# Spread reads on SyncE's queue, product sums dealt out over wave slots, attention of two batches at fixed waves

## The chip, the cores and the metric

The kernel runs on one core of one Trainium2 chip. The metric is the device time of a whole execution in microseconds: 318.45 us before the change, the median of 3 runs (317.96 to 318.91). The core has a matrix engine (TensorE, PE in the profile, with its weight loads as PEld), VectorE (DVE), ScalarE (ACT), GpSimd (POOL) and SyncE (SP), which here only issues transfers. Matrix products are written to PSUM, all other tiles lie in SBUF.

## The reference

Two blocks run one after the other. The first is an attention whose weights are products of two small projections. The second is a gated feed-forward layer.

```python
# attention: q, k, v are (4, 4, 1088, 32); S1, S2 are (8, 32)
a = np.einsum('rd,bhsd->bhsr', S1, x)            # phi(x), for x = q and x = k
b = np.einsum('rd,bhsd->bhsr', S2, x)
phi = np.einsum('bhsi,bhsj->bhsij', a, b).reshape(*x.shape[:-1], 64)
kv  = np.einsum('bhsf,bhsd->bhfd', k_p, v)
num = np.einsum('bhsf,bhfd->bhsd', q_p, kv)
den = np.einsum('bhsf,bhf->bhs', q_p, k_p.sum(axis=2))[..., None] + 1e-06
attn = num / den
# feed-forward: x is (4352, 128); w_gate, w_val are (128, 1536); w_out is (1536, 128)
x = attn.transpose(0, 2, 1, 3).reshape(4352, 128)
out = (1 / (1 + np.exp(-(x @ w_gate))) * (x @ w_val)) @ w_out
```

## The kernel before

**Feed-forward part.** The 4352 tokens are cut into chunks of 512 (numbers 0 to 7) and one of 256 (number 8). The 1536 hidden columns are cut into 12 blocks of 128. One *wave* (`w1`, matmuls at L457) multiplies a chunk by the gate and value weights of one block; ScalarE takes the sigmoid of the gate half (L465), and VectorE multiplies it with the value half (`glu`, L487, tile g). Waves write to a PSUM tile with two buffers. A chunk has 12 waves (chunk 8 has 6, of two blocks each), and waves are counted through all chunks: `moe["n"]`.

Chunks 1 to 7 form the product with w_out by a scheme of seven half-size products in place of eight (as Strassen and Winograd do it), over pairs of blocks. For each pair of waves GpSimd forms sums of the two g (`token_sums`, L328 to L335, tile tsum), and sums of the weights stand ready in ws. PE then runs four products into one accumulator in PSUM (`w2_a`, tag acc0) and three into another (`w2_b`, tag acc1), all at L339. There is one buffer for each tag. `w2_a` of a pair is put three, and `w2_b` four wave slots after that of the pair's second wave. After the last pair of a chunk, the results are combined: ScalarE copies the upper halves of each accumulator to SBUF (L401, L428), VectorE adds (L402 and L405 from acc0; L429 to L432 from acc1 and from tiles in SBUF), turns the result (L436, tile o_sb), and SyncE stores it (`store`, L353).

Chunks 0 and 8 use the plain product instead (`w2`, L370), into acc0 as their numbers are even.

**The order of work** is written out by hand. The order in the program is the order on each of the four compute engines. `slot(group, waves)` first emits a piece of attention work, and then, for each of so many waves: the `glu` of the wave before, the products that are due, and the matmuls of the next wave:

```python
        for _ in range(waves):
            ...
            glu()
            while todo and todo[0][0] <= moe["n"]:
                todo.pop(0)[1]()
            if more:
                w1()
```

The sums of a chunk's end are emitted inside the last `w2_a` and the last `w2_b`, behind the products.

**Attention part.** Batch 0 is done ahead of the waves. For batches 1 to 3 the pieces are, in order: `turn_k`, `turn_q` (transposes on VectorE, L536, L547), `begin` (projections kps and cqps on PE, then `spread`), `outer` twice (L646), `sum_z` twice (L822), `kv_all` (kvz on PE), `qmult` twice (L766, needs the tiles qp and bq), `weights_z` (L897 to L904), `ndt`, and `parts` (den_j, nps and the division, which writes the tokens xT that later waves read). Before, a loop over the batches puts one wave (batch 1) or two waves (batches 2 and 3) between the pieces.

`spread(b, ns, cq, put, get)` writes the projected queries cq to a DRAM tile dq (queue `put`) and reads them back in other layouts: six reads into qp and bq (queue `get`, L738) and eight into the small tiles a8 and b8 (queue `put`, L759). For batches 1 to 3 `put` is SyncE and `get` is GpSimd.

Of the kernel before, what the change touches and what calls it, by code (L numbers as in the profile page):

```python
# [12 lines left out]
ALU = mybir.AluOpType  # L13
# [7 lines left out]
def kernel(  # L21
# [282 lines left out]

    xT = const.tile([P, NTOK], F32, tag="xT")

    moe = {"sum": -1, "ci": 0, "w": 0, "n": 0, "ready": 0, "acc": None, "gate": None, "todo": []}

    def fast(ci):
        return 0 < ci < len(tok_chk) - 1 and tok_chk[ci][1] == TCH  # L310
# [77 lines left out]
    def w2_a(ci, i, g, t):  # L388
        if i == 0:
            moe["sum"] = ci  # L390
            fst["a"] = pso.tile([P, TCH], F32, tag="acc0", name="prod")
        lo, hi = fst["a"][:64], fst["a"][64:]
        w, first, last = w_sb[:, 2], i == 0, i == NJ // 2 - 1
        product(lo[:, :HALF], w[:, 2 * i, :64], g[:, 0, :HALF], first, last)
        product(hi[:, :HALF], w[:, 2 * i + 1, :64], g[:, 1, :HALF], first, last)
        product(lo[:, HALF:], ws[:, 3, i], g[:, 1, HALF:], False, last)
        product(hi[:, HALF:], ws[:, 1, i], t[:, 2], False, last)
        if last:
            e = fst["e"] = raw.tile([P, 2, 2, HALF], F32, tag="w_in", name="other")[:64]
            r = fst["r"] = raw.tile([P, 5, HALF], F32, tag="w_in", name="res")[:64]  # L400
            nc.scalar.copy(out=e[:, 0], in_=hi.rearrange("p (u x) -> p u x", u=2))  # L401
            nc.vector.tensor_tensor(  # L402
                out=ends(r, 1, 3), in0=twice(lo[:, :HALF]), in1=e[:, 0], op=ALU.add
            )
            nc.vector.tensor_tensor(out=r[:, 2], in0=lo[:, HALF:], in1=r[:, 4], op=ALU.add)  # L405

    def twice(x):
        return bass.AP(tensor=x.tensor, offset=x.offset, ap=[list(x.ap[0]), [0, 2], [1, HALF]])

    def ends(r, u, step):  # L410
        x = r[:, u]
        return bass.AP(
            tensor=x.tensor, offset=x.offset, ap=[list(x.ap[0]), [step * HALF, 2], [1, HALF]]
        )

    def w2_b(ci, i, g, t):
        if i == 0:
            fst["b"] = pso.tile([P, TCH], F32, tag="acc1", name="prod")
        lo, hi = fst["b"][:64], fst["b"][64:]
        w, first, last = w_sb[:, 2], i == 0, i == NJ // 2 - 1  # L420
        p5 = (lo[:, :HALF], ws[:, 0, i], t[:, 0], first, last)
        p4 = (hi[:, :HALF], w[:, 2 * i + 1, 64:], t[:, 3], first, last)
        p7 = ((hi if i % 2 else lo)[:, HALF:], ws[:, 2, i], t[:, 1], False, i >= NJ // 2 - 2)
        for p in (p4, p5, p7) if i % 2 else (p5, p4, p7):
            product(*p)
        if last:
            e, r = fst["e"], fst["r"]
            nc.scalar.copy(out=e[:, 1], in_=hi.rearrange("p (u x) -> p u x", u=2))  # L428
            nc.vector.tensor_tensor(out=r[:, 0], in0=lo[:, HALF:], in1=e[:, 1, 1], op=ALU.add)  # L429
            nc.vector.tensor_tensor(out=r[:, 4], in0=r[:, 4], in1=r[:, 0], op=ALU.add)  # L430
            nc.vector.tensor_tensor(out=r[:, 3], in0=r[:, 4], in1=e[:, 1, 0], op=ALU.subtract)
            nc.vector.tensor_tensor(  # L432
                out=ends(r, 2, 2), in0=twice(lo[:, :HALF]), in1=ends(r, 2, 2), op=ALU.add
            )
            o_sb = sbA.tile([P, 2, TCH // 32, 32], F32, tag="o_sb", name="o_sb")
            nc.vector.transpose(  # L436
                out=o_sb[:64].rearrange("p d t x -> p (d t x)"),
                in_=r[:, 1:].rearrange("p u x -> p (u x)"),
            )
            store(ci, lambda g4: o_sb[32 * (g4 % 2) : 32 * (g4 % 2) + 32, g4 // 2])  # L440

    def w1():

        ci = moe["ci"]
        t0, tw = tok_chk[ci]
        jn = TCH // tw
        j0 = moe["w"] * jn
        wv = psm.tile([P, 2, TCH], F32, tag="wave", name="wave")

        tp = tw // 2 if ci == 0 and j0 == 0 else tw  # L450
        turn = (moe["w"] // 2) % 2
        for o in range(0, tw, tp):
            for which in range(2):
                for jj in range(jn):
                    for c in (0,) if ci == 0 else (1 - turn, turn):
                        d = slice(0, P) if ci == 0 else slice(64 * c, 64 * c + 64)
                        nc.tensor.matmul(  # L457
                            out=wv[d, which, jj * tw + o : jj * tw + o + tp],
                            lhsT=w_sb[:, which, j0 + jj, d],
                            rhs=xT[:, t0 + o : t0 + o + tp],  # L460
                            start=True,
                            stop=True,
                        )
        sg = sbG.tile([P, TCH], F32, tag="sg", name="sg")
        nc.scalar.activation(out=sg, in_=wv[:, 0], func=ACTF.Sigmoid)  # L465
        if ci == 0:
            if j0 == 1:
                narrow_01(2, 3)
            if 0 < j0 < NJ - 2:
                narrow_w(j0 + 1, 3)  # L470
            narrow_w(j0 + 2, 1)
            narrow_w(j0 + 2, 2)
            if j0 < 3:
                narrow_w(j0 + 3, 0)
            if j0 > 1:
                narrow_w(j0 + 4, 0)
            if j0 == NJ - 3:
                weight_sums(0, NJ // 4)
        if ci == 1 and j0 == 1:
            weight_sums(NJ // 4, NJ // 2)  # L480
        if moe["w"] % 2 == 0:
            moe["g"] = sbG.tile([P, 2, TCH], F32, tag="g", name="g")
        pair, odd, n = moe["g"], moe["w"] % 2, moe["n"]

        def glu():
            g = pair[:, odd]
            nc.vector.tensor_tensor(out=g, in0=wv[:, 1], in1=sg, op=MUL)  # L487
            todo = moe["todo"]
            if not fast(ci):
                lag = 3 if ci else 2  # L490
                part = (ci, j0, jn, g.rearrange("p (j t) -> p j t", j=jn))
                todo.append((n + lag, lambda: w2(*part)))
            elif odd:
                part = (ci, j0 // 2, pair, token_sums(pair))
                todo.append((n + 3, lambda: w2_a(*part)))
                todo.append((n + 4, lambda: w2_b(*part)))

        moe["gate"] = glu
        moe["w"] += 1
        moe["n"] += 1  # L500
        if j0 + jn == NJ:
            moe["ci"] += 1
            moe["w"] = 0

    def glu():
        if moe["gate"] is not None:
            moe["gate"]()
            moe["gate"] = None

    def slot(group, waves):  # L510

        if group is not None:
            group()
        todo = moe["todo"]
        for _ in range(waves):
            more = moe["ci"] < len(tok_chk)
            if more and sum(tok_chk[moe["ci"]]) > moe["ready"]:
                break
            glu()
            while todo and todo[0][0] <= moe["n"]:  # L520
                todo.pop(0)[1]()
            if more:
                w1()
            elif not todo:
                break
            else:
                todo.pop(0)[1]()
# [236 lines left out]
    def qmult(b, n):  # L764
        q0 = half(QP[b], n)
        nc.vector.tensor_tensor(out=q0, in0=q0, in1=half(BQ[b], n), op=MUL)  # L766
# [368 lines left out]
    def begin(b):  # L1135
        glu()
        kps(b)
        cq[b] = qcomp(b, (0, 1), (psm, "wave"))
        spread(b, (0, 1), cq[b], nc.sync, nc.gpsimd)

    def q01():
        spread(0, (1,), qcomp(0, (1,), (ps2, "two")), nc.scalar, nc.sync)
# [24 lines left out]
    def kv_all(b):  # L1167
        kv(b, ZS[b])
        kvd(b)
# [8 lines left out]
    slot(lambda: part01(lambda: narrow_w(NJ - 1, 3)), 1)  # L1178
    slot(last01, 1)
    v_t[1] = load_v(1)  # L1180
    for b in range(1, B):
        more = b + 1 < B
        wn = 1 if b == 1 else 2
        turn_k(b)
        if b > 1:
            turn_q(b, 0)
        slot(None, wn)
        if b == 1:
            turn_q(b, 0)
        turn_q(b, 1)  # L1190
        slot(lambda: begin(b), 1)
        for pi in range(2):
            outer(b, pi)
            slot(None, wn)
        for step in range(2):
            sum_z(b, step)
            slot(None, wn)
            if b == 1 and step == 0:
                masks()
        slot(lambda: kv_all(b), wn)  # L1200
        if more:
            v_t[b + 1] = load_v(b + 1)
        qmult(b, 0)
        weights_z(b)
        slot(lambda: ndt(b), 1)
        qmult(b, 1)
        load_kq(b + 1)
        if b == 1:
            slot(None, 1)
        slot(lambda: parts(b), wn + 5)  # L1210
    slot(None, 10**3)


# [28 lines left out]
```

## Time and profile before

| what | value |
|---|---|
| time, median of 3 runs | 318.45 us |
| profiled execution: span, mean granted PE clock | 318.3 us, 0.972 |
| waves L457 on PE | 820 records, 215.8 us busy |
| products L339 on PE | 588 records, 153.7 us busy (68.8 + 33.9 + 26.0 + 25.0) |
| g, L487 on VectorE | 102 of 684 ns, 69.7 us busy |
| token sums L328, L334, L335 on GpSimd | 42 each of 1377, 753 and 815 ns |
| chain that ended last | PE 64%, DVE 14%, POOL 10%, issue 6%, DMA 2%, ACT 2% |
| reads qp<-dq and bq<-dq on GpSimd's queue | 18, median 8.1 and 9.5 us from issue to landing |
| chunk sums on VectorE, mean of one | L402 681, L405 416, L429 411, L430 416, L431 416, L432 682, L436 1236 ns |

Busy time on PE overlaps with itself, as matmuls are pipelined. The clock is a share of full speed, as the throttle grants it. In the list of waits a row says which engine and line waited, for which engine and line, and gives the total in us, the number of times, and the longest. In the timeline a row gives the start in us, the duration, the engine, line and operation, the tiles (out<-in), the shapes, how many instructions were merged, and in brackets how long the engine was idle before it, and for whom.

### The profile page before, as it was taken

Reading aid. Unit: us, or ns where it says so; the run is one execution under the profiler, and the core shown is the slowest. Engines: PE = TensorE matmul, PEld = TensorE weight load, DVE = VectorE, ACT = ScalarE, POOL = GpSimd, SP = SyncE. Lnnn points to the kernel's source line nnn. Section 1 sums busy time; section 2 is a strip of 40 time slices with the busy share of each in tenths; the row PEclk is TensorE's granted clock in tenths of the full one; section 3 lists DMA queues with packets and bytes.
Section 4 is the critical chain, followed back from the end, with each engine's and each line's share of the span. In section 5 each row is a group of like instructions: output and inputs, shape, how many; then the busy total and the mean of one; then the engine's idle time right before and its main releaser. Section 6 shows DMA issues by size and latency. Waiting matters only on the chain.

```text
span 318.3 us, 5511 instructions
## 1 busy us (share of the span) xinstructions
PE 299.3 (94%) x2176; PEld 153.6 (48%) x2176; DVE 184.9 (58%) x310; ACT 88.8 (28%) x164; POOL 161.6 (51%) x196
## 2 busy tenths in 40 slices
PE   9899999499999889979999999899999999999995
PEld 3444432145454344533654455443555456545853
DVE  6997798817629546386255954795226422832361
ACT  2556523112124122230223312221223222322320
POOL 1456560954453694603546976434554655466300
PEclk9999999879999799995999999999999999999999
DMA  7994142963300394215000790002000200010021
GB/s 219 353 309 105 69 141 55 215 139 97 121 0 0 84 229 99 61 26 163 2 0 37 159 211 5 2 1 35 1 0 2 33 0 2 4 31 0 0 35 17
DMA packets 30553, 24.35 MB, mean 76 GB/s; under 512 B 20480, under 2 KB 25728, under 8 KB 30528
## 3 DMA queue, kind: packets, MB, share of 16 engines
q1 hardware_dynamic: 27024, 16.15, 19.1%
q0 software_dynamic: 2592, 7.08, 9.6%
q10 hardware_dynamic: 912, 0.77, 0.9%
q8 instruction: 17, 0.28, 0.4%
q14 instruction: 8, 0.07, 0.1%
HBM read 20.73 MB, written 3.26 MB: 75 GB/s over the span
## 4 chain that ended last, share of the span: by engine, by line
PE 64%; DVE 14%; POOL 10%; issue 6%; DMA 2%; ACT 2%; SPq 0%; POOLq 0%; ACTq 0%; DVEq 0%
PE wave L457 40%; PE prod L339 16%; POOL head L118 3%; POOL tsum L328 2%; PE moeout L370 2%; POOL ws L323 2%; DVE head L109 2%; DVE g L487 2%; PE nps L982 2%; DVE w_sb L127 1%; DVE o_sb L436 1%; POOL bq L738 1%; POOL tsum L334 1%; PE kvz L788 1%; DMA dq<-cq 1%
## 5 line engine op out<-in xcount | busy, mean ns | idle before, releaser
L457 PE MATMUL wave<-xT,w_sb 128*64 128x512 f32 (+3 forms) x820 | 215.8, 577 | 0.8 <-DVE g L487 0.8
L487 DVE TENSOR_TENSOR g<-wave,sg 128x512 f32<-128x512 f32 x102 | 69.7, 684 | 111.6 <-ACT sg L465 107.3
L457 PEld LDWEIGHTS wave<-xT,w_sb 128*64 128x64 f32 (+1 forms) x820 | 83.3, 143 | 71.0 <-issue 52.4
L465 ACT ACTIVATE sg<-wave 128x512 f32<-128x512 f32 x102 | 61.0, 598 | 196.4 <-PE wave L457 189.0
L328 POOL TENSOR_TENSOR tsum<-g 128x512 f32<-128x512 f32 x42 | 57.8, 1377 | 97.6 <-DVE g L487 97.6
L339 PE MATMUL prod<-tsum,ws 128*64 128x256 f32 x252 | 68.8, 391 | 6.6 <-POOL tsum L334 6.6
L339 PEld LDWEIGHTS prod<-tsum,ws 128*64 128x64 f32 x252 | 33.4, 140 | 21.6 <-issue 8.5
L335 POOL TENSOR_TENSOR tsum<-tsum,g 128x256 f32<-128x256 f32 x42 | 34.2, 815 | 3.3
L339 PE MATMUL prod<-g,w_sb 128*64 128x256 f32 x168 | 33.9, 382 | 0.1
L334 POOL TENSOR_TENSOR tsum<-tsum,g 128x256 f32<-128x256 f32 x42 | 31.6, 753 | 3.3
L339 PE MATMUL prod<-tsum,w_sb 128*64 128x256 f32 x84 | 26.0, 392 | 0.0
L339 PE MATMUL prod<-g,ws 128*64 128x256 f32 x84 | 25.0, 379 | 0.0
L339 PEld LDWEIGHTS prod<-g,w_sb 128*64 128x64 f32 x168 | 16.0, 137 | 18.1 <-issue 16.9
L118 POOL TENSOR_TENSOR head<-head,tail 128x384 int32<-128x384 int32 (+2 forms) x14 | 13.3, 953 | 18.0 <-DVE head L109 14.9
L370 PE MATMUL moeout<-g,w_sb 128*128 128x512 f32 (+1 forms) x48 | 18.9, 503 | 0.3 <-DVE w_sb L127 0.3
L339 PEld LDWEIGHTS prod<-tsum,w_sb 128*64 128x64 f32 x84 | 11.3, 139 | 7.8 <-issue 6.8
L339 PEld LDWEIGHTS prod<-g,ws 128*64 128x64 f32 x84 | 11.5, 137 | 3.3
L370 PEld LDWEIGHTS moeout<-g,w_sb 128*128 128x128 f32 x48 | 8.5, 189 | 8.3 <-issue 4.2
L646 DVE TENSOR_TENSOR kp<-kab 128x1152 f32<-128x1152 f32 (+2 forms) x10 | 11.3, 1144 | 0.0
L766 DVE TENSOR_TENSOR qp<-qp,bq 128x1152 f32<-128x1152 f32 (+1 forms) x7 | 9.1, 1296 | 0.0
L982 PE MATMUL nps<-qp,nd 64*32 64x256 f32 (+1 forms) x128 | 6.5, 465 | 2.6 <-DVE qp L766 2.3
L436 DVE STREAM_TRANSPOSE o_sb<-res 64x1024 f32<-64x1024 f32 x7 | 8.7, 1236 | 0.2
(114 smaller groups left out, 196.0 us busy)
## 6 DMA issues: line engine op xcount, KB each, us to landing
qp<-dq POOLq DMA_DIRECT2D x6, 576.0 KB, 8.1
bq<-dq POOLq DMA_DIRECT2D x12, 288.0 KB, 9.5
v<-in_v_dram SPq DMA_DIRECT2D x16, 144.0 KB, 3.9
kq<-in_k_dram SPq DMA_DIRECT2D x3, 544.0 KB, 4.1
kq<-in_q_dram SPq DMA_DIRECT2D x3, 544.0 KB, 5.0
w_in<-in_moe_w_out_dram SPq DMA_DIRECT2D x6, 256.0 KB, 7.1
w_in<-in_moe_w_gate_dram SPq DMA_DIRECT2D x5, 256.0 KB, 6.1
w_in<-in_moe_w_val_dram SPq DMA_DIRECT2D x5, 256.0 KB, 6.6
```

The lines of the kernel that those rows point to most:

```text
L118: nc.gpsimd.tensor_tensor(out=head, in0=head, in1=tail, op=ALU.add)
L328: nc.gpsimd.tensor_tensor(out=t[:, :2], in0=g.rearrange("p f (t x) -> p t f x", t=2)[:, 1], in1=g1, op=ALU.subtract,)
L334: nc.gpsimd.tensor_tensor(out=t[:, 2], in0=t[:, 1], in1=g1[:, 0], op=ALU.add)
L335: nc.gpsimd.tensor_tensor(out=t[:, 3], in0=t[:, 2], in1=g[:, 1, :HALF], op=ALU.subtract)
L339: nc.tensor.matmul(out=out, lhsT=lhsT, rhs=rhs, start=start, stop=stop, skip_group_check=True)
L370: nc.tensor.matmul(out=moe["acc"][:, :tw], lhsT=w_sb[:, 2, j, :], rhs=g[:, jj, :tw], start=(j == 0), stop=(j == NJ - 1),)
L436: nc.vector.transpose(out=o_sb[:64].rearrange("p d t x -> p (d t x)"), in_=r[:, 1:].rearrange("p u x -> p (u x)"),)
L457: nc.tensor.matmul(out=wv[d, which, jj * tw + o : jj * tw + o + tp], lhsT=w_sb[:, which, j0 + jj, d], rhs=xT[:, t0 + o : t0 + o + tp], sta ...
L465: nc.scalar.activation(out=sg, in_=wv[:, 0], func=ACTF.Sigmoid)
L487: nc.vector.tensor_tensor(out=g, in0=wv[:, 1], in1=sg, op=MUL)
L646: eng.tensor_tensor(out=KP[b][:, pi, j0:j1].rearrange("p j m (i l) -> p (j m) i l", i=R), in0=bass.AP(tensor=a0.tensor, offset=a0.offset, ...
L982: nc.tensor.matmul(out=t[32 * h : 32 * h + 32, c, :w], lhsT=ND[b][rows, 32 * h : 32 * h + 32], rhs=half(QP[b], n)[rows, 2 * (h % 2) + h // ...
```

## The change

It has three parts. The six reads of `spread` for batches 1 to 3 are issued by SyncE, so that GpSimd has no transfer to wait for or to issue. The sums at a chunk's end become a list of steps, `moe["late"]`, of which one is emitted in each wave slot, behind its `glu` and ahead of the products that are due; the aim is that VectorE has no long run of work in one slot. They are also regrouped: L431's subtraction comes first, the last two additions become one, and the transpose is done in two halves. Chunk 8's first product waits one slot longer. Third, the attention pieces of batches 2 and 3 are each put at a wave number (`plan`), apart from the ends of chunks; batch 1 keeps its order.

```diff
         if last:
...
-            nc.vector.tensor_tensor(
-                out=ends(r, 1, 3), in0=twice(lo[:, :HALF]), in1=e[:, 0], op=ALU.add
-            )
-            nc.vector.tensor_tensor(out=r[:, 2], in0=lo[:, HALF:], in1=r[:, 4], op=ALU.add)
+            def first_sums():
+                add(ends(r, 1, 3), twice(lo[:, :HALF]), e[:, 0])
+            def third():
+                add(r[:, 2], lo[:, HALF:], r[:, 4])
+            moe["late"] += [[first_sums], [third]]
...
-            nc.vector.tensor_tensor(out=r[:, 0], in0=lo[:, HALF:], in1=e[:, 1, 1], op=ALU.add)
-            nc.vector.tensor_tensor(out=r[:, 4], in0=r[:, 4], in1=r[:, 0], op=ALU.add)
-            nc.vector.tensor_tensor(out=r[:, 3], in0=r[:, 4], in1=e[:, 1, 0], op=ALU.subtract)
-            nc.vector.tensor_tensor(
-                out=ends(r, 2, 2), in0=twice(lo[:, :HALF]), in1=ends(r, 2, 2), op=ALU.add
-            )
...
+            def fourth():
+                add(r[:, 3], r[:, 4], e[:, 1, 0], op=ALU.subtract)
+            def fifth():
+                add(ends(r, 2, 2), twice(lo[:, :HALF]), ends(r, 2, 2))
+            def seventh():
+                add(r[:, 0], lo[:, HALF:], e[:, 1, 1])
+            def last_sums():
+                add(r[:, 3:5], r[:, 3:5], twice(r[:, 0]))
...
+            def turn_store():
+                turned(1)
+                store(ci, lambda g4: o_sb[32 * (g4 % 2) : 32 * (g4 % 2) + 32, g4 // 2])
+            moe["late"] += [[fourth, fifth, seventh], [last_sums], [lambda: turned(0)], [turn_store]]
...
-                lag = 3 if ci else 2
+                lag = 2 if ci == 0 else 3 if j0 else 4
...
             glu()
+            for step in moe["late"].pop(0) if moe["late"] else ():
+                step()
             while todo and todo[0][0] <= moe["n"]:
                 todo.pop(0)[1]()
...
-        spread(b, (0, 1), cq[b], nc.sync, nc.gpsimd)
+        spread(b, (0, 1), cq[b], nc.sync, nc.sync)
...
+    plan = {2: (27, 29, 30, 31, 32, 34, 36, 37, 38, 39, 42, 44)}
+    plan[3] = (48, 49, 51, 53, 56, 57, 58, 59, 60, 61, 63, 68)
+    for b in range(2, B):
+        at = iter(plan[b])
+        until(next(at))
         turn_k(b)
+        for n in range(2):
+            until(next(at))
+            turn_q(b, n)
+        until(next(at))
         slot(lambda: begin(b), 1)
...
```

More of the change, by code (lines that the diff above doesn't have):

```diff
@@ L305 @@
     xT = const.tile([P, NTOK], F32, tag="xT")
-    moe = {"sum": -1, "ci": 0, "w": 0, "n": 0, "ready": 0, "acc": None, "gate": None, "todo": []}
+    moe = {"sum": -1, "ci": 0, "w": 0, "n": 0, "ready": 0, "acc": None, "gate": None, "todo": [], "late": []}
     def fast(ci):
@@ L401, in w2_a, with add @@
             nc.scalar.copy(out=e[:, 0], in_=hi.rearrange("p (u x) -> p u x", u=2))
-            nc.vector.tensor_tensor(
-                out=ends(r, 1, 3), in0=twice(lo[:, :HALF]), in1=e[:, 0], op=ALU.add
-            )
-            nc.vector.tensor_tensor(out=r[:, 2], in0=lo[:, HALF:], in1=r[:, 4], op=ALU.add)
+            def first_sums():
[3 more added lines that the diff above has]
+            moe["late"] += [[first_sums], [third]]
+    def add(out, in0, in1, op=ALU.add):
+        nc.vector.tensor_tensor(out=out, in0=in0, in1=in1, op=op)
     def twice(x):
@@ L428, in w2_b, with turned @@
             nc.scalar.copy(out=e[:, 1], in_=hi.rearrange("p (u x) -> p u x", u=2))
-            nc.vector.tensor_tensor(out=r[:, 0], in0=lo[:, HALF:], in1=e[:, 1, 1], op=ALU.add)
-            nc.vector.tensor_tensor(out=r[:, 4], in0=r[:, 4], in1=r[:, 0], op=ALU.add)
-            nc.vector.tensor_tensor(out=r[:, 3], in0=r[:, 4], in1=e[:, 1, 0], op=ALU.subtract)
-            nc.vector.tensor_tensor(
-                out=ends(r, 2, 2), in0=twice(lo[:, :HALF]), in1=ends(r, 2, 2), op=ALU.add
-            )
-            o_sb = sbA.tile([P, 2, TCH // 32, 32], F32, tag="o_sb", name="o_sb")
[L436 to L440, printed above, removed]
+            o_sb = sbA.tile([P, 2, TCH // 32, 32], F32, tag="o_sb", name="o_sb")
+            def fourth():
[6 more added lines that the diff above has]
+                add(r[:, 3:5], r[:, 3:5], twice(r[:, 0]))
+            def turned(d):
+                nc.vector.transpose(
+                    out=o_sb[:64, d].rearrange("p t x -> p (t x)"),
+                    in_=r[:, 1 + 2 * d : 3 + 2 * d].rearrange("p u x -> p (u x)"),
+                )
+            def turn_store():
+                turned(1)
+                store(ci, lambda g4: o_sb[32 * (g4 % 2) : 32 * (g4 % 2) + 32, g4 // 2])
+            moe["late"] += [[fourth, fifth, seventh], [last_sums], [lambda: turned(0)], [turn_store]]
     def w1():
@@ L1180, with until @@
     v_t[1] = load_v(1)
-    for b in range(1, B):
-        more = b + 1 < B
-        wn = 1 if b == 1 else 2
-        turn_k(b)
[L1185 to L1190, printed above, removed]
+    turn_k(1)
+    slot(None, 1)
+    turn_q(1, 0)
+    turn_q(1, 1)
+    slot(lambda: begin(1), 1)
+    for pi in range(2):
+        outer(1, pi)
+        slot(None, 1)
+    for step in range(2):
+        sum_z(1, step)
+        slot(None, 1)
+        if step == 0:
+            masks()
+    slot(lambda: kv_all(1), 1)
+    v_t[2] = load_v(2)
+    qmult(1, 0)
+    weights_z(1)
+    slot(lambda: ndt(1), 1)
+    qmult(1, 1)
+    load_kq(2)
+    slot(None, 1)
+    slot(lambda: parts(1), 1)
+    def until(n):
+        slot(None, n - moe["n"])
+    plan = {2: (27, 29, 30, 31, 32, 34, 36, 37, 38, 39, 42, 44)}
[3 more added lines that the diff above has]
+        until(next(at))
+        turn_k(b)
+        for n in range(2):
+            until(next(at))
+            turn_q(b, n)
+        until(next(at))
         slot(lambda: begin(b), 1)
         for pi in range(2):
+            until(next(at))
             outer(b, pi)
-            slot(None, wn)
         for step in range(2):
+            until(next(at))
             sum_z(b, step)
[L1197 to L1201, printed above, removed]
+        until(next(at))
+        slot(lambda: kv_all(b), 1)
+        if b + 1 < B:
             v_t[b + 1] = load_v(b + 1)
+        until(next(at))
         qmult(b, 0)
+        slot(lambda: ndt(b), 1)
         weights_z(b)
-        slot(lambda: ndt(b), 1)
+        until(next(at))
         qmult(b, 1)
         load_kq(b + 1)
-        if b == 1:
-            slot(None, 1)
-        slot(lambda: parts(b), wn + 5)
+        until(next(at))
+        slot(lambda: parts(b), 1)
     slot(None, 10**3)
```

## The prediction

> **What bounds the kernel now.** I read the engine shares and the slices first, then the waits, then stretches of the timeline. The page:
>
> ```profile
> PE 299.3 (94%) x2176; PEld 153.6 (48%) x2176; DVE 184.9 (58%) x310; ACT 88.8 (28%) x164; POOL 161.6 (51%) x196
> ...
> PEclk9999999879999799995999999999999999999999
> ```
>
> TensorE (PE) is the bound, at 94%; the busy time of the others is no limit. Each slice is 8 us; slices 8, 14 and 19 (from 1) show that PE also ran at less than full clock. From about 218 us on nothing is lost (81.80 busy of 82.00 us below): the twelve waves of a chunk take 29.74 us (a wave that starts at 228.36 in the chain comes again at 258.10). So time can only be won between 49 and 218 us, where the attention of batches 1 to 3 is mixed in. The list of waits says where:
>
> ```profile
> POOL qp L738 <- DMA dq<-cq: 9.7, 2, 7.7
> ...
> PE prod L339 <- POOL tsum L334: 6.6, 3, 5.2
> ...
> PE nps L982 <- DVE qp L766: 2.3, 2, 1.2
> PE cqps L713 <- DVE qT L547: 1.7, 1, 1.7
> PE denj L917 <- ACT sg L465: 1.3, 1, 1.3
> ```
>
> GpSimd (POOL) stood 7.7 us in front of a read of dq whose write had not landed; its token sums came late, and PE waited 5.2 us for them. The other waits fall where VectorE (DVE) has a chunk's sums and attention work in one lump. What idleness does to the clock (columns: window; its length; busy us of PE, PEld, DVE, ACT, POOL; PE clock; DMA):
>
> ```profile
> 57.88:61.29 3.41, 1.36 (x10) 0.46 (x6) 3.38 (x7) 0.60 (x1) 3.25 (x5) 1.00 0.94 221
> 64.70:68.12 3.42, 3.42 (x11) 1.21 (x11) 0.00 (x0) 0.00 (x0) 3.26 (x6) 0.50 1.02 223
> 105.67:109.08 3.41, 3.41 (x13) 1.47 (x13) 1.70 (x2) 0.62 (x1) 2.21 (x2) 0.50 0.46 121
> 114.20:117.60 3.40, 2.43 (x17) 1.21 (x15) 2.30 (x2) 0.60 (x1) 3.24 (x4) 1.00 0.99 219
> 218.00:300.00 82.00, 81.80 (x512) 46.76 (x514) 31.18 (x48) 21.94 (x37) 46.35 (x51) 1.00 0.07 11
> ```
>
> After a stretch of 3.41 us in which PE was busy 1.36 us the clock was halved; after one with 2.43 us busy it was not.
>
> [...]
>
> **The change, part by part.**
> 1. *Reads issued by SyncE.* POOL no longer waits for dq nor issues 18 reads (about 0.55 us each in the timeline). Of the PE time in batch 1 this frees 5.2 us idle, and 1.8 us of the half-clock stretch to 68.12 that fell on work (half of 68.12 - 64.45): 7.0. In batch 2 it frees 1.0 (PE's wait for tsum at 115.5), in batch 3 0.6 (PE's waits at 180 to 184, where POOL also issues). Behind the waiting reads on SyncE stand the a and b reads and stores; they land some 2.5 us later (6 issues of about 0.43). I cost that at nothing: qmult, den_j and their data have several waves of 2.4 us of room, and stores have two buffers.
> 2. *Fixed waves.* Begin and parts of batches 2 and 3 move away from the sums of a chunk. Frees: around 103 us 1.7 idle and 1.7 of halved clock; around 140 to 150 us 1.3 + 1.2 idle, 1.2 by which nps took longer than in batch 3 (2.87 against 1.7) and 1.7 of halved clock, together 5.4; around 206 and 218 us 1.1 + 0.7. Sum of 1 and 2: 7.0 + 1.0 + 0.6 + 3.4 + 5.4 + 1.7 = 19.1. The whole loss of the stretch is a little more; I leave the rest where it is.
> 3. *Sums dealt out.* This is where I choose against the change. There is one acc0 and one acc1. A chunk's last w2_a runs in wave slot s, its last w2_b in s+1; the next chunk's first w2_a needs acc0 in s+2, its first w2_b acc1 in s+3. Before, all sums are put on VectorE in s and s+1:
>
> ```profile
> 242.24 0.42 DVE L405 TENSOR_TENSOR res<-prod,res 64x256 f32<-64x256 f32 x1
> ...
> 243.19 1.88 PE L457 MATMUL wave<-xT,w_sb 128*64 128x512 f32 x7
> ...
> 244.53 0.75 PE L339 MATMUL prod<-g,w_sb 128*64 128x256 f32 x3
> ...
> 245.35 0.68 DVE L432 TENSOR_TENSOR res<-prod,res 64x512 f32<-64x512 f32 x1
> ...
> 247.11 0.59 PE L339 MATMUL prod<-tsum,ws 128*64 128x256 f32 x2
> ```
>
> acc0 is read out at 242.66 and taken again at 244.53; acc1 at 246.03 and 247.11: 1.9 and 1.1 us to spare. After, `third`, the last reader of acc0, is put in slot s+2 behind that slot's glu, directly ahead of the w2_a that needs it; `fourth, fifth, seventh` in s+3, behind its glu, directly ahead of the w2_b that needs acc1. The order of the changed program's instructions shows both: on PE, wave, a wait for `third`, products, wave, a wait for `seventh`, products. A glu can't run before its own wave is over:
>
> ```profile
> 249.70 0.60 PE L339 MATMUL prod<-g,w_sb 128*64 128x256 f32 x4
> 249.92 0.60 ACT L465 ACTIVATE sg<-wave 128x512 f32<-128x512 f32 x1 [1.62 <-PE wave L457]
> ...
> 250.55 0.69 DVE L487 TENSOR_TENSOR g<-wave,sg 128x512 f32<-128x512 f32 x1 [1.46 <-ACT sg L465]
> ```
>
> Products that wait for nothing start at 249.70; the g of the wave ahead ends at 251.24, 1.54 us later (1.6 elsewhere). So PE stands 1.58 + 0.03 (gap) + 0.42 (L405's duration) + 0.07 (VectorE's end to PE's start; 0.05 at 143.75, 0.15 at 104.84) = 2.1 us in s+2, and 1.58 + 0.42 + 0.68 + 0.42 (L430, L432, L429) + 3 x 0.03 + 0.07 = 3.3 us in s+3. All other work is queued behind them on PE, so nothing hides them. Six chunk ends (1 to 2 up to 6 to 7) pay both: 6 x 5.4 = 32.4. The end of chunk 7 pays the first alone, as chunk 8's products use acc0: 2.1.
> 4. *Clock.* [...] Bounds: nothing, or two half-clock windows for a chunk end (3.4 lost). I take one, 3.41 / 2 = 1.7: 6 x 1.7 = 10.2.
> 5. *End.* The second half of chunk 7's output is turned after chunk 8's, and three more stores are issued behind it, at 0.43 us each: 1.3. The extra VectorE instructions (31 by the order) lie beside PE and cost nothing.
>
> Sum: 318.45 - 19.1 + 32.4 + 2.1 + 10.2 + 1.3 = 345.35; I say 345.
>
> **Rivals.**
> - *A, the lumps go and the chunk ends stay free:* 318.45 - 19.1 + 1.3 = 300.7. For it: VectorE idles 111.6 us ahead of g, so spreading costs it nothing. Against: the order of the two waits. It needs g to run earlier than its wave allows. 10%, with part-hidden gaps that end near 320 another 3%.
> - *B, the gaps come but the clock holds:* 345.35 - 10.2 = 335. For it: 2.43 of 3.40 busy kept the clock, and products and a wave (2.6 us) run between the two gaps. 22%.
> - *C, both gaps halve the clock at each end:* 345.35 + 10.2 = 355.5. For it: the stretch 143 to 150 stayed slow for two windows. 15%.
> - *Forecast, one slow window at each end:* 345. 50%.
>
> **Numbers.** Range 331 to 356: B's 335 less the 4 us by which the freed 19.1 may be short of the real loss, up to C. Left out are A (13% with the part-hidden) and some 6% above C. Chances: faster 0.10, within 0.3% 0.01, slower 0.89: only A and its neighbours are not slower.
>
> **What would show it.** Right: in the changed profile PE prod waits for DVE res, 13 times, about 2.1 and 3.3 us in turn, seven chunk ends apart by some 37 us instead of 29.74; half-clock slices spread over the whole second half; VectorE's lumps gone; PE prod no longer waiting 5.2 us for tsum, and no dq wait on POOL. Wrong: products at chunk ends that start as soon as their wave is through; or waits of qp multiplications or pd for DMA, which would make part 1 false; or the clock at 1.0 over the second half, which is B.

## The result, and the profile after

The changed kernel takes 341.2 us (median of 4 runs, 337.84 to 342.61) against 318.68 us before (317.96 to 319.07); the ratio is 1.069, with a 95% interval of 1.061 to 1.078. It is slower by 22.5 us. One kernel's runs fall into two states, and only those of the faster one are compared: of the seven runs of the kernel before beside the first four experiments, three of over 321 us, at clock 0.972, are left out.

PE's share of busy time fell from 94% to 88% in a longer span, with the same 2176 matmul records (page of the changed kernel):

```profile
PE 301.0 (88%) x2176; PEld 158.3 (46%) x2176; DVE 187.4 (55%) x317; ACT 88.8 (26%) x164; POOL 155.7 (46%) x178
...
PEclk9999999999998999899999999989997999899999
```

The half-clock slices no longer end with the attention; they reach into the second half. What PE waited for, the changed kernel's list (total us, times, longest):

```profile
PE prod L339 <- DVE res L412: 28.2, 12, 3.0
PE moeout L370 <- DVE res L412: 1.8, 1, 1.8
PE prod L339 <- POOL tsum L334: 1.6, 2, 1.2
```

The old waits for tsum (6.6 us), qp, qT and denj are gone or small, and the wait for dq on POOL is gone. In their place stands one cause, the sums of a chunk (res; L412 is the helper that all these additions now go through). Together these are 30.0 us in 13 waits. (A wait of 3.0 us for res is also booked on the weight loads; it is the same gap as PE's 2.5 at the end of chunk 3, and doesn't count again.) One end of a chunk in the timeline, with no attention near it (end of chunk 6):

```profile
285.20 1.94 PE L477 MATMUL wave<-xT,w_sb 128*64 128x512 f32 x8
...
287.17 0.60 ACT L485 ACTIVATE sg<-wave 128x512 f32<-128x512 f32 x1 [0.98 <-PE wave L477]
287.80 0.69 DVE L507 TENSOR_TENSOR g<-wave,sg 128x512 f32<-128x512 f32 x1 [0.84 <-ACT sg L485]
288.41 0.41 DVE L412 TENSOR_TENSOR res<-prod,res 64x256 f32<-64x256 f32 x1
...
288.96 0.65 PE L339 MATMUL prod<-g,w_sb 128*64 128x256 f32 x4 [1.83 <-DVE res L412]
...
289.85 1.92 PE L477 MATMUL wave<-xT,w_sb 128*64 128x512 f32 x8
...
291.82 0.60 ACT L485 ACTIVATE sg<-wave 128x512 f32<-128x512 f32 x1 [4.05 <-PE wave L477]
292.52 0.69 DVE L507 TENSOR_TENSOR g<-wave,sg 128x512 f32<-128x512 f32 x1 [3.70 <-ACT sg L485]
293.13 0.41 DVE L412 TENSOR_TENSOR res<-res,other 64x256 f32<-64x256 f32 x1
293.57 0.68 DVE L412 TENSOR_TENSOR res<-prod,res 64x512 f32<-64x512 f32 x1
294.18 0.41 DVE L412 TENSOR_TENSOR res<-prod,other 64x256 f32<-64x256 f32 x1
...
294.73 0.40 PE L339 MATMUL prod<-tsum,ws 128*64 128x256 f32 x1 [2.96 <-DVE res L412]
```

Read it as two loops through three engines: wave on PE, sigmoid on ACT, g on DVE, then the sums behind g, and only then the next products on PE. A wave at full clock takes PE 1.72 us (257.88 to 259.60 in the kernel before, where the products behind it wait for nothing), so the first wave's slot ends at 286.92 and the products start 2.04 us later; the second ends at 291.57 and its products start 3.16 us later. (The brackets and the list give about 0.2 less, because they count from the modelled end of the last matmul. By start times all 13 gaps make 7 x 2.04 + 5 x 3.16 + 2.5 = 32.6 us.) After the second gap the clock drops to 0.50, at 295.46. Two of the five half-clock stretches of the changed kernel (window; length; busy us of PE, PEld, DVE, ACT, POOL; PE clock; DMA):

```profile
141.87:145.28 3.41, 3.41 (x12) 1.42 (x9) 0.47 (x1) 0.00 (x0) 0.00 (x0) 0.50 0.53 153
...
295.47:298.88 3.41, 3.41 (x12) 1.28 (x9) 0.00 (x0) 0.00 (x0) 0.00 (x0) 0.50 0.00 0
```

A chunk now takes 36.40 us (products behind the first gap at 252.56 and again at 288.96), against 29.74 before: 2.04 + 3.16 of waiting, and the rest, 1.5, halved clock.

### The profile page after: what moved, and what is told of

Read it like the earlier page. It is cut to its first block, busy times and chain, and to the rows that moved or that the text cites. A ratio compares the mean times of both kernels' runs of the same rounds, so it can differ in the third digit from the quotient of the medians.

```text
span 340.6 us, 5502 instructions
## 1 busy us (share of the span) xinstructions
PE 301.0 (88%) x2176; PEld 158.3 (46%) x2176; DVE 187.4 (55%) x317; ACT 88.8 (26%) x164; POOL 155.7 (46%) x178
## 4 chain that ended last, share of the span: by engine, by line
PE 73%; DVE 9%; DMA 8%; POOL 4%; ACT 3%; issue 2%; SPq 1%; DVEq 0%; POOLq 0%
PE wave L477 47%; PE prod L339 19%; DVE g L507 3%; DVE res L412 3%; PE moeout L370 3%; ACT sg L485 3%; DMA v<-in_v_dram 3%; DMA w_in<-in_moe_w_out_dram 2%; DMA bq<-dq 2%; POOL tsum L328 2%; DMA w_in<-in_moe_w_gate_dram 1%; PE nps L1004 1%; POOL head L118 1%; PE kvz L810 1%; POOL tsum L334 1%
## 5 line engine op out<-in xcount | busy, mean ns | idle before, releaser
L477 PE MATMUL wave<-xT,w_sb 128*64 128x512 f32 (+3 forms) x820 | 218.3, 582 | 0.0
L328 POOL TENSOR_TENSOR tsum<-g 128x512 f32<-128x512 f32 x42 | 63.1, 1503 | 133.2 <-DVE g L507 133.1
L477 PEld LDWEIGHTS wave<-xT,w_sb 128*64 128x64 f32 (+1 forms) x820 | 88.2, 143 | 66.7 <-issue 46.4
L339 PE MATMUL prod<-tsum,ws 128*64 128x256 f32 x252 | 65.8, 392 | 18.9 <-DVE res L412 17.3
L339 PEld LDWEIGHTS prod<-tsum,ws 128*64 128x64 f32 x252 | 31.7, 140 | 36.9 <-issue 26.2
L339 PE MATMUL prod<-g,w_sb 128*64 128x256 f32 x168 | 35.2, 392 | 11.0 <-DVE res L412 11.0
L339 PEld LDWEIGHTS prod<-g,w_sb 128*64 128x64 f32 x168 | 16.9, 142 | 32.3 <-issue 30.0
L451 DVE STREAM_TRANSPOSE o_sb<-res 64x512 f32<-64x512 f32 x14 | 9.6, 688 | 0.0
L127 DVE SCALAR_TENSOR_TENSOR w_sb<-square,head 128x384 f32<-128x384 f32 (+1 forms) x11 | 5.7, 518 | 3.9 <-POOL head L118 3.9
```

Of the source, the lines that this page charges most:

```text
L328: nc.gpsimd.tensor_tensor(out=t[:, :2], in0=g.rearrange("p f (t x) -> p t f x", t=2)[:, 1], in1=g1, op=ALU.subtract,)
L339: nc.tensor.matmul(out=out, lhsT=lhsT, rhs=rhs, start=start, stop=stop, skip_group_check=True)
L451: nc.vector.transpose(out=o_sb[:64, d].rearrange("p t x -> p (t x)"), in_=r[:, 1 + 2 * d : 3 + 2 * d].rearrange("p u x -> p (u x)"),)
L477: nc.tensor.matmul(out=wv[d, which, jj * tw + o : jj * tw + o + tp], lhsT=w_sb[:, which, j0 + jj, d], rhs=xT[:, t0 + o : t0 + o + tp], sta ...
```

## The experiments

Each was timed beside the kernel before, whose median was 317.7 us for the first four (four runs, 316.79 to 319.01) and 317.8 us for the last four (seven runs). Gains are counted from these. The changed kernel was not timed again: its 341.2 us are those of the first comparison.

**Each part alone.** First, only the reads moved.

```diff
-        spread(b, (0, 1), cq[b], nc.sync, nc.gpsimd)
+        spread(b, (0, 1), cq[b], nc.sync, nc.sync)
```

> The kernel before, with only the spread reads of batches 1 to 3 moved from GpSimd's to SyncE's queue. Theory (the slowdown comes from accumulators that are set free late; the reads are a gain): 318.7 - (7.0 + 1.0 + 0.6) = about 310, and PE's wait for tsum falls from 6.6 us to under 1. Rival 1 ([...]SyncE's queue only moves the wait from GpSimd to the multiplications that need bq): within 2 us of 318.7. Rival 2 (the reads on SyncE cause the slowdown): over 325.

Measured: 308.9 us, ratio 0.972 (0.966 to 0.979). Both rivals fall: the reads are a gain of 8.8 us, and PE's wait for tsum is 1.6 us (under 1 was expected). The size hides a surprise. The waits for qp, qT and denj are all still there, but no stretch of the profiled run was at half clock (its mean clock is 1.00). Three windows of this kernel, in which the waits lie that stood around 103 and 140 to 144 us before:

```profile
97.09:100.50 3.41, 1.72 (x36) 0.42 (x34) 3.38 (x6) 0.60 (x1) 1.34 (x2) 1.00 0.26 40
131.22:134.64 3.42, 2.08 (x15) 0.68 (x11) 3.35 (x7) 0.60 (x1) 0.08 (x1) 1.00 0.07 10
134.64:138.05 3.41, 2.25 (x46) 0.98 (x48) 3.09 (x7) 0.00 (x0) 3.25 (x3) 1.00 0.41 63
```

This work came 5 to 8 us earlier, and the same waits fell elsewhere in time; the last section comes back to it.

Then the changed kernel with the old sums, which is the kernel before with the other two parts:

```diff
-        spread(b, (0, 1), cq[b], nc.sync, nc.gpsimd)
+        spread(b, (0, 1), cq[b], nc.sync, nc.sync)
...
+    plan = {2: (27, 29, 30, 31, 32, 34, 36, 37, 38, 39, 42, 44)}
+    plan[3] = (48, 49, 51, 53, 56, 57, 58, 59, 60, 61, 63, 68)
...
```

> The changed kernel with the chunk sums put back as they were (all in the last w2_a and w2_b; chunk 8's first lag 3 again); reads on SyncE and the fixed waves stay. Theory: both other parts are gains, 318.7 - 19.1 = about 300, no wait of PE for res, no half-clock stretch between 60 and 290 us. Rival (reads on SyncE or the fixed waves make the loss, and the sums are harmless): 335 or more. Rival (each part costs some): 318 to 330.

Measured: 302.4 us, ratio 0.953 (0.949 to 0.957). PE has no wait for res; 1.5 us for tsum and 1.2 us for g are left. Between 60 and 290 us no stretch is at half clock. So reads and plan together are worth 15.3 us, and dealing out the sums turns this faster kernel into a slower one.

Only the sums, on the kernel before:

```diff
+            moe["late"] += [[first_sums], [third]]
...
+            moe["late"] += [[fourth, fifth, seventh], [last_sums], [lambda: turned(0)], [turn_store]]
```

> The kernel before, with only the sums dealt out over six slots. Theory: the whole loss of the chunk ends (6 x 5.2 + 2.1, about 8 of halved clock, 1.3 at the end: some 43) on top of 318.7, less up to 10 where VectorE's lumps near 103, 140 and 215 us get smaller: 350 to 362. Rival (dealing out is a gain wherever VectorE is crowded, and the loss comes from the fixed waves): under 325.

Measured: 351.1 us, ratio 1.106 (1.102 to 1.111), inside the theory's range. PE waits 30.5 us for res in 12 waits, the longest 5.0 us, where a chunk end meets the attention; the 5.2 us for tsum stay.

Only the plan, on the kernel before:

```diff
-        wn = 1 if b == 1 else 2
...
+    plan = {2: (27, 29, 30, 31, 32, 34, 36, 37, 38, 39, 42, 44)}
+    plan[3] = (48, 49, 51, 53, 56, 57, 58, 59, 60, 61, 63, 68)
```

> The kernel before, with only the fixed waves for batches 2 and 3; reads stay on GpSimd and the sums in one lump. Theory: the lumps of VectorE no longer meet attention, 318.7 - (3.4 + 5.4 + 1.7) = about 308; the 5.2 us wait for tsum near 60 us stays. Rival (the plan gains nothing without dealt sums, or moves attention into new collisions): 318 to 325.

Measured: 313.0 us, ratio 0.986 (0.982 to 0.990): a gain of 4.7, not 10.5. The half-clock stretches around 105 and 143 us are gone. But as long as GpSimd issues the reads, it waits for dq at the new places too. Its own wait grew from 9.7 to 11.7 us, and PE's wait for tsum from 6.6 to 8.7. Rows of this kernel's lists of waits, of POOL and of PE:

```profile
POOL qp L738 <- DMA dq<-cq: 11.7, 3, 7.8
```

```profile
PE prod L339 <- POOL tsum L334: 8.7, 4, 5.3
PE wave L457 <- DVE g L487: 1.2, 3, 0.5
```

Reads and plan alone add up to 13.5 us, and together they gave 15.3; together, POOL's wait for dq is gone at the new places too.

**Which order does it.** Now only the place of the dealt steps is changed, against the changed kernel; the instructions are the same. First `third` alone, ahead of its slot's `glu`:

```diff
+            steps = moe["late"].pop(0) if moe["late"] else ()
+            ahead = [x.__name__ for x in steps] == ["third"]
+            for step in steps if ahead else ():
+                step()
             glu()
-            for step in moe["late"].pop(0) if moe["late"] else ():
+            for step in () if ahead else steps:
                 step()
```

> The changed kernel with one of the dealt steps moved: third (the last reader of acc0) is emitted ahead of its slot's glu instead of behind it; nothing else. Theory: PE's first wait at each chunk end (2.0 us by the trace) goes, the second (3.2 us) stays, and so do the half-clock windows, as all five follow the second wait: 341.2 - 7 x 2.05 = about 327, PE's waits for res 6 times instead of 13. Rival (both gaps together lower the clock): 327 - 8 = about 319. Rival (the wait is not the order behind glu): 341.

Measured: 331.8 us, against 341.2 for the changed kernel. The gain of 9.4 is smaller than the 14 expected. The trace shows why: `first_sums` still stands behind the glu of the slot before, so `third` can end at 281.78 only, and the products start at 281.92 instead of 281.28. The first gap shrank from 2.04 us to between 0.5 and 0.64 and did not vanish: 327 + 7 x 0.6 = 331.2. Four half-clock stretches stayed, at the second gap of four chunk ends.

Then the other group, with the same edit and another condition:

```diff
+            steps = moe["late"].pop(0) if moe["late"] else ()
+            ahead = len(steps) == 3
...
```

> The changed kernel with fourth, fifth and seventh (the readers of acc1) emitted ahead of their slot's glu, and third left behind it. Theory: the second wait goes at five of the six chunk ends (at the end of chunk 3 a begin emits glu first, there it stays) and with it the half-clock windows: 341.2 - 5 x 3.2 - 5 x 1.5 = about 318, at least 13 less than third moved alone. Rival (the clock follows from the number of gaps, not the longer one): the slow windows stay in part, 320 to 325.

Measured: 320.1 us, so 21.1 faster than the changed kernel, and 11.8 faster than with `third` moved (at least 13 was expected). The time lies between the theory's 318 and the lower end of the rival's range, so it can't decide; the trace does. The first gaps stay (six of 1.8 us and one of 2.5 at the end of chunk 3 in the list of waits), and one half-clock stretch is left between 60 and 310 us, at 171.3: at the end of chunk 3, where both gaps stay. Five gaps of 2.0 us that stood alone never halved the clock. So at these chunk ends it is the 3.2 us gap that the halved clock follows.

All steps ahead:

```diff
-            glu()
             for step in moe["late"].pop(0) if moe["late"] else ():
                 step()
+            glu()
```

> The changed kernel with all dealt steps emitted ahead of their slot's glu. Theory: the 2.0 us waits go. The readers of acc1 now stand behind the glu of the wave before, done 1.6 + 1.6 us after that wave, while PE reaches the next w2_b after 0.86 + 1.72 = 2.6 us: 0.6 to 0.7 us of wait is left at each of five ends, 2 to 2.5 at the end of chunk 3. Sum: 300 + 1.6 + 5 x 0.7 + 2.5 = about 307, no slow windows. Rival (dealing out is bad in itself, as it adds VectorE instructions): over 318.

Measured: 309.5 us, ratio 0.973 (0.969 to 0.976), from two lines that change places: 31.7 us faster than the changed kernel. Waits for res are 5.3 us in 6. The rival, that dealing out is bad in itself, falls. It is 2.5 us over the 307 expected: at the end of chunk 1 a piece of attention (`turn_q`) stands ahead of the sums too, and the wait is 1.6 us, and behind the 2.5 us gap at the end of chunk 3 one stretch of 3.41 us is at half clock. At the other four ends the residue is as worked out, about 0.7 us by start times: `seventh` is behind the g of the wave before, and PE comes by a little too early (row of this kernel's timeline):

```profile
265.36 0.40 PE L339 MATMUL prod<-tsum,ws 128*64 128x256 f32 x1 [0.29 <-DVE res L412]
```

Last, with the steps ahead of `glu` as in the experiment before, and both accumulators read out one slot earlier:

```diff
-            moe["late"] += [[fourth, fifth, seventh], [last_sums], [lambda: turned(0)], [turn_store]]
+            moe["late"][0] += [fourth, fifth, seventh]
+            moe["late"] += [[last_sums], [lambda: turned(0)], [turn_store]]
```

> The changed kernel with the dealt steps ahead of glu, and third, fourth, fifth and seventh together in the slot behind first_sums, so that both accumulators are read out one slot earlier; the last sums and the two half transposes stay dealt out over three more slots. Theory: no wait for res at all, and VectorE's lump is 1.9 us instead of 3.2: 299 to 302, faster than both kernels and within 2 us of the changed kernel with the old sums (which tells what dealing out is worth). Rival (the waits come back on g, since four sums stand ahead of it): 305 or more.

Measured: 298.7 us, ratio 0.940 (0.937 to 0.942): faster than both kernels, and no wait for res at all. The same place as above in its timeline:

```profile
252.63 0.41 DVE L412 TENSOR_TENSOR res<-prod,res 64x256 f32<-64x256 f32 x1
252.96 0.41 DVE L412 TENSOR_TENSOR res<-res,other 64x256 f32<-64x256 f32 x1
253.25 0.79 PE L339 MATMUL prod<-g,w_sb 128*64 128x256 f32 x4
253.47 0.68 DVE L412 TENSOR_TENSOR res<-prod,res 64x512 f32<-64x512 f32 x1
...
254.08 0.41 DVE L412 TENSOR_TENSOR res<-prod,other 64x256 f32<-64x256 f32 x1
...
254.41 0.67 DVE L508 TENSOR_TENSOR g<-wave,sg 128x512 f32<-128x512 f32 x1
...
255.83 0.38 PE L339 MATMUL prod<-tsum,ws 128*64 128x256 f32 x1
```

acc0 is read out at 253.04 and its products start at 253.25, right when the wave ahead (from 251.53) is through; acc1 is free at 254.49 and taken at 255.83. The four sums now stand ahead of a g, which starts a little late and harms nobody. It beats the old sums with the same reads and plan (ratio 0.940 against 0.953, intervals apart) by about 3.8 us: that is what dealing out is worth, with the regrouping that came with it, once nothing waits for it. (Within 2 us was expected.)

## Why the prediction was right, point by point

**The waits at the chunk ends (32.4 + 2.1)** were the step that carried the sign, and it held: 13 waits, 2.04 and 3.16 us where 2.1 and 3.3 were worked out, 32.6 us by start times for 34.5. Nothing hid them: the wave behind the first gap's products started at 289.85, after the last of them (289.67). Experiments 5 to 8 show the cause, not only the place: with the same instructions, moving steps ahead of glu takes the waits away one by one. The end of chunk 3 was cheaper than the others (2.5 against 3.0 us): kps and cqps ran inside its second gap.

**Clock (10.2).** Five half-clock stretches in six ends. With the waiting part of two of them taken off, 8.2 us were lost (half of 3.20 + 3 x 3.41 + 3.00). The missing one is again the end of chunk 3. That one stretch per end would be slow was the author's estimate, a choice between bounds, and that it came so near is in part luck: by their mean clocks, the four runs of the changed kernel lost between 3.7 and 8.9 us. Case C, both gaps, is refuted by the five stretches themselves, at most one for each end, and by experiment 6. Between the forecast's two cases (1.36 and 2.43 us busy) lies a third that it left out: in the kernel before, the half clock from 105.67 us on follows 3.41 us with 1.72 us of PE busy. (Its page has four slices below full clock, 8, 9, 14 and 19, of which 8 and 9 are one stretch.)

```profile
102.26:105.67 3.41, 1.72 (x36) 0.58 (x36) 3.41 (x6) 0.62 (x2) 1.50 (x2) 1.00 0.31 47
```

**What is freed (19.1)** was too much: reads and plan gave 15.3. The term that was mis-sized is the plan's 10.5, of which it gave 4.7 alone, for two reasons. POOL's waits moved along and cost PE 2.1 us more for tsum. And the profile that the forecast read is of a run of 320.05 us at clock 0.972, while the runs of the kernel before that are compared here have clocks of 0.982 to 0.989: (1 - clock) times the span, an estimate of the work lost, is 8.9 us in the first and 3.5 to 5.7 in the others. So part of the halved clock that was counted as freed was not there to be won in most runs. That this closes the sum is worked out from the clocks, not tried. The reads gave 8.8 for 8.6, but not as counted: PE's wait of 5.2 us fell to 1.2 and not to nothing, and the halved clock around 103 and 143 us went without the plan.

**Dealing out costs and brings nothing beside the waits:** wrong by 3.8 us, its gain with early release. That this error and the one before cancel (15.3 + 3.8 = 19.1 against 19.1) is luck. The pages count 7 more VectorE instructions (317 against 310), not 31.

**The end (1.3):** from the last moeout to the end of the span it is 5.4 us (335.19 to 340.6) against 3.8 before, so 1.6. With early release it is 3.7.

Put together from the kernel with early release: 298.7 + 32.6 + 8.2 + 1.6 = 341.1. The median is 341.2; the profiled run, from which the waits and the clock are taken, took 342.4, so some 1.3 us of it stay unexplained. The forecast's 345.35 lay 4.2 us above this sum: by the waits (1.9), the clock (2.0) and the start (318.45 - 19.1 = 299.35 against 298.7, 0.65), less 0.3 at the end.

**Rivals.** Case A would have been right about the gain, 300.7, had the accumulators been free; experiment 8 is that case (298.7). The other sign of being wrong, waits for the reads on SyncE, hardly showed: a qp multiplication waited for bq once, for 2.0 us, and PE's list has no wait for it.

## What to carry to other kernels

Spreading a lump of work over later slots also moves the moment at which its inputs come free: here from 1.9 us ahead of acc0's next products to a wait of 2.04 us. Ask of each piece whether it is the last reader of a buffer that another engine takes again, and put it ahead of anything that waits for that engine's current work. A gain and a loss in one change hide each other: here two parts were worth about 15 us, and the third hid them behind 38.8.

## What the runs showed of the hardware

- The halved clock followed some gaps of a length and not others. Of gaps of 2.0 us that stood alone it followed none (five in experiment 6). Of gaps of 3.2 us it followed most: all five in the profiled run of the changed kernel (the sixth end has the shorter gap of 2.5), four of five with the first gap shortened (experiment 5), two of four with the sums alone (experiment 3). In experiment 1 the waits of the kernel before, only 5 to 8 us earlier, halved nothing, though they had halved it twice; one of these two was a lone wait of 1.7 us.
- In the 3.41 us just ahead of each of the five half-clock stretches of the changed kernel, PE was busy for 0.64 to 1.10 us. At the end of chunk 3, where the clock held, two stretches of that length had 2.45 and 1.90. One of each kind, and one with a lone gap of experiment 6, behind which the clock held too (changed kernel, ahead of the last half-clock stretch and at the end of chunk 3; then experiment 6):

```profile
292.05:295.46 3.41, 0.73 (x7) 0.63 (x9) 2.03 (x4) 0.36 (x1) 0.00 (x0) 1.00 0.00 0
179.41:182.82 3.41, 1.90 (x13) 1.03 (x15) 1.42 (x4) 0.00 (x0) 0.00 (x0) 1.00 0.35 97
```

```profile
236.11:239.52 3.41, 1.84 (x9) 0.65 (x5) 2.18 (x4) 1.34 (x3) 1.30 (x3) 1.00 0.00 0
```

- The same work went both ways: half clock followed the 1.72 us busy of the kernel before at 102.26, and in experiment 1 the clock held behind the 1.72 at 97.09. The waits around 140 us of the kernel before left PE busy for 1.45 us between 139.80 and 143.21, and half clock followed; in experiment 1 they lie in two stretches with 2.08 and 2.25, and the clock held. Why 1.72 went both ways is not shown by these runs.
- The changed kernel's own time is uneven, and its clock with it. Its four runs have mean clocks of 0.974, 0.989, 0.974 and 0.985. (1 - clock) times the span, the same estimate as above, gives 8.9 us lost at 342.37 and 3.7 at 337.84. The difference of 5.2 is about that of the times, 4.5. Early release, at clock 0.999 to 1.0, lies within 0.8 us.
